# Segment-recurrent attention: Q, K and softmax worked in place, 23 streamed weight pieces, the mask added by a matmul

## The chip, the cores and the metric

The kernel runs on one core of a Trainium2 chip. The metric is device time in microseconds. The kernel before takes 1896.9 us, the median of three runs from 1884.9 to 1905.76. Five engines of the core matter here: TensorE (PE in the profile, its weight loads PEld), VectorE (DVE), ScalarE (ACT), GpSimd (POOL), and SyncE (SP), which only issues transfers. Sixteen DMA engines move the data.

## The reference

Two independent attentions on 2048 rows of 640 columns each, with outputs side by side. Part A is a dilated sliding window: 32 heads of 20, each row attends to 8 rows at distance 2. Part B, which the change concerns, is recurrent over 64 segments of 32 rows:

```python
for s in range(n_seg):                       # 64 segments of 32 rows
    h = concat([mem, x[segment s]])          # 8 memory rows + 32 rows = 40
    q, k, v = h @ Wq, h @ Wk, h @ Wv         # 32 heads of 192
    scores = where(mask, q @ k.T * Dh**-0.5, -1e9)
    o = softmax(scores) @ v
    o = o @ Wo                               # back to 640 columns
    mem = o[:8]; outs.append(o[8:])
```

The mask lets memory rows see all 40 rows, and other rows see rows up to themselves. A segment needs the first 8 output rows of the segment before it, so the 64 segments run one after the other. Wq, Wk, Wv and Wo are 640 x 6144 in bf16, 7.9 MB each, more than the on-chip memory holds together.

## The kernel before, in words

**Stages.** Part A runs first (line 24), with part B's resident weights loading beside it. Then 64 segments of part B. In the end project_late (line 782) makes the outputs for the last 8 rows of each segment, which are computed one segment late.

**Weights.** They are cut into pieces: 5 for each of four head groups of q, k and v (128 x 1536, 384 KB), and 24 for the output (128 x 1280, 320 KB). Most stay in SBUF for the whole of part B. Those named in STREAMED (line 285) do not fit: 8 of k, 10 of v and 6 of o, 24 in all, are read from device memory anew in each segment, through a ring of seven buffers, one transfer a piece, issued by SyncE in the order of use (fetch, line 434). A transfer is issued when the piece seven places ahead in the ring has been used.

**Rows.** In a segment the current 32 rows stand in HX as "main"; "ahead" holds the last 8 rows of four coming segments, which are independent of the recurrence. Each k and v group is projected from "ahead" once in four segments (RENEW, line 288) and q for one group a segment (token ql); such a group gets a second pass of 20 matmuls, and its four sets of 8 late columns are kept in small blocks (Lb) until their segment.

**One segment** runs through four head groups. Order on TensorE, VectorE, ScalarE and SyncE is written out by hand, as a list of tokens (ORDER, line 297); each engine takes its own instructions from the tokens in that order. The tokens, for a group g:

- q.g, k.g, v.g: projections (line 512), 20 matmuls of 384 columns, four side by side in the array, into one of three PSUM "acc" buffers.
- e.: copies acc out of PSUM as bf16 (line 518), on ScalarE (S) or VectorE (V) by EVACUATE, into one of three "sb" buffers.
- T.: VectorE transposes 32 x 32 blocks from sb into the columns 0 to 31 of each head third of QT or KT (line 522), while POOL puts the late columns into 32 to 39 (lines 538, 554). There is one QT and one KT, which all groups use in turn.
- S.g: scores, 16 small matmuls into a bank of PSUM (line 573).
- sb.g: VectorE scales the scores, adds the mask and writes them to an SBUF tile t (line 580). mx.g: maximum. sub.g: subtract it and take exp on ScalarE (lines 591, 592). send.g: sum, reciprocal, and the products that write P (lines 596, 597, 606).
- tp.g: P transposed by two matmuls with the identity (line 613). PT.g: VectorE multiplies it with a 0/1 column pair "own" (line 619).
- ve.g: values out of PSUM to Vst, and of a second pass to LV (lines 562, 564). mix.g: P times values (line 632). ot.g: to OT (line 640), by HEADS.
- out.g.h: the output projection of groups 0 to 2, accumulated in Y (line 660); last: that of group 3 (line 687).
- tx: the next segment's rows into HX. ql, eql, Tql: the q projection of the late rows. part, join, close: the halves of Y added, and the next segment's memory rows written into HX (line 694), with which q.0 of the next segment begins. The output rows leave by POOL's queue (line 697).

A PSUM buffer, QT or KT is written anew when the last reader of its former content is done.

Of the kernel before, what the change touches and what calls it, by code (L numbers as in the profile page):

```python
# [23 lines left out]
def part_a(ctx, tc, A_x, A_wqkv, A_wo, out, ident, emit_loads):  # L24
# [241 lines left out]
    with tc.manual_schedule(engines={mybir.EngineType.PE, mybir.EngineType.DVE, mybir.EngineType.Activation}):  # L266
# [4 lines left out]
        for b in range(-1, n_blk):  # L271
# [13 lines left out]
STREAMED = {"q": ((), (), (), ()), "k": ((0, 2), (2, 3), (1, 4), (0, 4)), "v": ((0, 3), (0, 2), (1, 2, 4), (0, 2, 4)),  # L285
            "o": (8, 13, 16, 18, 22, 23)}
SLOT = 1536
RENEW = {0: ("k0", "v2"), 1: ("k1", "v3"), 2: ("k2", "v0"), 3: ("k3", "v1")}
BLOCKS = 18
FIRST = """  # L290
    q.0 e.q0 T.q0 k.0 e.k0 T.k0 q.1 e.q1 k.1 S.0 sb.0 T.q1 e.k1 mx.0 sub.0 T.k1 send.0 q.2 e.q2 v.0 ve.0
    S.1 sb.1 tp.0 PT.0 T.q2 k.2 e.k2 T.k2 mx.1 sub.1 mix.0 ot.0 v.1 ve.1 send.1 S.2 sb.2 out.0.0 out.0.1
    tp.1 mx.2 sub.2 PT.1 q.3 e.q3 T.q3 k.3 send.2 e.k3 T.k3 mix.1 ot.1 v.2 ve.2 tp.2 PT.2 out.1.0 S.3
    sb.3 mx.3 sub.3 out.1.1 mix.2 ot.2 send.3 v.3 ve.3 out.2.0 tp.3 PT.3 tx out.2.1 part mix.3 ot.3 join
    ql eql last close Tql
# [21 lines left out]
def part_b(ctx, tc, B_x, B_mem0, B_Wq, B_Wk, B_Wv, B_Wo, out, ident, n_seg, pre, nbuf, mid):  # L317
# [26 lines left out]

    copied = {}

    def copy_streamed():

        for m, g in need:
            for u in pieces(m, g):  # L350
                if streamed(u):
                    copied[u] = dpool.tile([128, unit_cols(u)], BF16, name="wcopy_%s%d_%d" % u)[:]
                    nc.sync.dma_start(two_rows(copied[u], u), unit_src(u))
# [4 lines left out]
    for m, g in need:  # L358
        resident += [u for u in pieces(m, g) if not streamed(u)]
    res, wait = {}, set()  # L360

    def place_resident(pool, units):
        for u in units:
            res[u] = pool.tile([128, unit_cols(u)], BF16, name="wres_%s%d_%d" % u)[:]

    def load_resident(units):
        for u in units:
            nc.sync.dma_start(two_rows(res[u], u), unit_src(u))

    n_pre, used = 0, 0  # L370
    while n_pre < len(resident) and used < pre:
        used += 2 * unit_cols(resident[n_pre])
# [49 lines left out]
    qk_sb = pool("b_qk", bufs=3)  # L422
# [11 lines left out]
    def fetch(u):  # L434
        t = wstream.tile([128, SLOT], BF16, tag="ws")
        nc.sync.dma_start(t[:, 0:unit_cols(u)], copied[u])
# [485 lines left out]
```

## Time and profile before

| | |
|---|---|
| median of three runs | 1896.9 us |
| the profiled execution | 1895.51 us |
| its span, first to last instruction | 1893.5 us |
| TensorE busy | 1650.9 us, 87% |
| VectorE busy | 1243.6 us, 66% |
| ScalarE busy | 714.6 us, 38% |
| GpSimd busy | 687.2 us, 36% |
| moved by DMA | 649.28 MB |

Busy is the time in which an engine has an instruction of its own in work. Matmul ends are modelled in the profile, so that TensorE's busy time is somewhat generous. The DMA digits of the page give the mean busy share of the 16 DMA engines in forty equal slices of the span, in tenths, 9 meaning 90% or more. A line of waits names the waiting engine and line, an arrow, what ended the wait, and then the total in us, how often, and the longest. "issue" stands where the profile shows nothing that the engine waited for. A line of operations gives count, busy time, mean time of one in ns, and the engine's idle time just before.

### The profile page before, as it was taken

The page shows a single profiled execution, that of the slowest core. Times are in us where ns is not written, and L with a number is a line of the kernel's source. Part 1 is how long each engine was busy: PE and PEld are TensorE (multiplying, and loading weights), DVE is VectorE, ACT ScalarE, POOL GpSimd, SP SyncE. Part 2 cuts the span into 40 slices and gives each one's busy share as a digit, 9 for nine tenths or more (in the row PEclk, how much of TensorE's full clock was granted, in tenths as well). Part 3 has the DMA queues.
Part 4 walks back from the last instruction along what each step waited for, and adds up shares of the span by engine and source line. Part 5 has one row for each costly group of instructions (what it writes and reads, how often), then busy time and mean ns, then how long its engine had stood idle before and what let it go on. Part 6 is the DMA issues. An engine that isn't in the chain of part 4 may idle for free.

```text
span 1893.5 us, 91779 instructions
## 1 busy us (share of the span) xinstructions
PE 1650.9 (87%) x39286; PEld 1031.8 (54%) x39286; DVE 1243.6 (66%) x3544; ACT 714.6 (38%) x1820; POOL 687.2 (36%) x1864
## 2 busy tenths in 40 slices
PE   8897898888898888888888888888888898888878
PEld 5565555555555555555555555555555555555558
DVE  4786676666666666667667667667666676666630
ACT  4454333334343333333333333343333333333320
POOL 3001344343343434433434334344443344444320
PEclk9999999999999999999999999999999999999999
DMA  9927899999999999999999999999999999999991
GB/s 328 320 72 262 312 379 364 360 358 365 373 366 368 360 369 360 358 361 364 357 364 368 365 340 369 365 360 366 373 371 366 358 382 365 343 365 368 356 370 45
DMA packets 286356, 649.28 MB, mean 343 GB/s; under 512 B 61140, under 2 KB 76946, under 8 KB 285948
## 3 DMA queue, kind: packets, MB, share of 16 engines
q1 hardware_dynamic: 267036, 630.01, 91.8%
q0 software_dynamic: 18400, 13.08, 2.2%
q8 instruction: 308, 5.05, 1.1%
q14 instruction: 100, 0.82, 0.1%
q10 hardware_dynamic: 512, 0.33, 0.1%
HBM read 629.10 MB, written 23.24 MB: 345 GB/s over the span
## 4 chain that ended last, share of the span: by engine, by line
PE 60%; DMA 22%; DVE 8%; issue 5%; ACT 3%; SPq 1%; ACTq 0%; POOL 0%; DVEq 0%
PE acc L512 33%; DMA t<-wcopy_v 13%; PE Y L660 6%; PE px L573 5%; DMA t<-wcopy_k 4%; DMA t<-wcopy_o 4%; PE px L632 3%; PE px L687 3%; PE pq L95 3%; PE px L613 2%; PE px L796 1%; DVE prod L151 1%; ACT part L667 1%; PE po L161 1%; ACT OT L640 1%
## 5 line engine op out<-in xcount | busy, mean ns | idle before, releaser
L512 PEld LDWEIGHTS <-HX 128*32 128x32 bf16 x19380 | 494.1, 97 | 416.7 <-issue 132.0
L512 PE MATMUL acc<-t,HX 128*32 128x384 bf16 x5812 | 434.2, 331 | 51.4 <-DMA t<-wcopy_v 30.5
L518 ACT CAST sb<-acc 128x384 bf16<-128x384 f32 x562 | 256.9, 476 | 429.9 <-PE acc L512 405.1
L512 PE MATMUL acc<-wres_q,HX 128*32 128x384 bf16 x6460 | 331.8, 330 | 58.9 <-DVE HX L694 43.5
L512 PE MATMUL acc<-wres_k,HX 128*32 128x384 bf16 x3876 | 246.0, 329 | 6.3 <-issue 5.9
L554 POOL COPY QT<-Lb 128x96 bf16<-128x96 bf16 x252 | 67.6, 268 | 476.0 <-PE px L573 475.8
L512 PE MATMUL acc<-wres_v,HX 128*32 128x384 bf16 x3232 | 225.6, 328 | 4.7 <-issue 4.6
L660 PE MATMUL Y<-wres_o,OT 128*32 128x320 bf16 x3840 | 212.0, 305 | 6.4 <-issue 6.0
L641 POOL COPY OL<-OT 128x96 bf16<-128x96 bf16 x256 | 157.8, 617 | 149.9 <-ACT OT L640 73.0
L619 DVE TENSOR_TENSOR PT<-px,own 128x320 bf16<-128x320 f32 x256 | 125.1, 489 | 105.6 <-PE px L613 51.9
L640 ACT CAST OT<-px 128x240 bf16<-128x240 f32 x384 | 126.1, 365 | 179.6 <-PE px L632 142.7
L592 ACT ACTIVATE t<-t 128x160 f32<-128x160 f32 x256 | 86.1, 336 | 242.1 <-DVE t L591 240.5
L562 ACT CAST Vst<-acc 128x384 bf16<-128x384 f32 x256 | 123.6, 483 | 142.8 <-PE acc L512 71.6
L642 POOL DMA_DIRECT2D late_o<-OL x256 | 139.4, 544 | 81.5 <-POOL OL L641 74.2
L522 DVE STREAM_TRANSPOSE QT<-sb 128x384 bf16<-128x384 bf16 x256 | 146.6, 573 | 17.0 <-PE px L573 14.6
L573 PE MATMUL px<-KT,QT 64*64 64x40 bf16 (+1 forms) x4096 | 139.2, 189 | 19.7 <-issue 9.8
L580 DVE SCALAR_TENSOR_TENSOR t<-px,mask 128x160 f32<-128x160 f32 x256 | 80.2, 313 | 110.5 <-PE px L573 104.1
L522 DVE STREAM_TRANSPOSE KT<-sb 128x384 bf16<-128x384 bf16 x256 | 143.8, 562 | 12.1 <-ACT sb L518 12.0
L573 PEld LDWEIGHTS <-QT 64*64 64x64 bf16 (+1 forms) x4096 | 109.3, 109 | 74.3 <-issue 42.1
L660 PEld LDWEIGHTS <-OT 128*32 128x32 bf16 x4608 | 114.6, 97 | 57.9 <-issue 15.7
L640 DVE CAST OT<-px 128x240 bf16<-128x240 f32 x128 | 51.8, 405 | 132.3 <-PE px L632 123.8
L697 POOL DMA_DIRECT2D out_dram<-XS x256 | 129.2, 511 | 22.4 <-DVE XS L695 15.6
(97 smaller groups left out, 2231.8 us busy)
## 6 DMA issues: line engine op xcount, KB each, us to landing
t<-wcopy_v SPq DMA_DIRECT2D x640, 384.0 KB, 6.2
t<-wcopy_k SPq DMA_DIRECT2D x512, 384.0 KB, 5.9
t<-wcopy_o SPq DMA_DIRECT2D x396, 320.0 KB, 5.7
wres_q<-in_B_Wq_dram SPq DMA_DIRECT2D x20, 384.0 KB, 7.9
late_o<-OL POOLq DMA_DIRECT2D x256, 24.0 KB, 5.1
wres_q<-late_o SPq DMA_DIRECT2D x16, 384.0 KB, 7.3
wres_o<-in_B_Wo_dram SPq DMA_DIRECT2D x18, 320.0 KB, 7.5
wres_k<-in_B_Wk_dram SPq DMA_DIRECT2D x12, 384.0 KB, 8.0
```

The lines of the kernel that those rows point to most:

```text
L512: nc.tensor.matmul(ps[n][32 * j:32 * j + 32].rearrange("p (f n) -> p f n", n=32), lhsT=X[:, dc, :], rhs=columns(w, m, j), start=(dc == 0), ...
L518: copy(sb[:], p[:])
L522: nc.vector.transpose(dst, sb[:].rearrange("p (f n) -> p f n", n=32))
L562: S_(Vst[:], ps[-1][:])
L573: nc.tensor.matmul(Sps[64 * h:64 * h + 64, a, :], lhsT=QT[k0:k1, L * f:L * f + 64], rhs=KT[k0:k1, f, :], start=(outer == 0 and a == 0), st ...
L592: nc.scalar.activation(t1[:], t1[:], ACTF.Exp)
L619: nc.vector.tensor_tensor(PT[:], pt.rearrange("p l (h n) -> p (l h) n", h=2)[:, :, 0:L].unsqueeze(2) .to_broadcast([128, 4, 2, L]), own[:] ...
L640: copy(OT[:, 6 * r:6 * r + 6].rearrange("p c n -> p (c n)"), ps[r][:, 0:6 * L])
L641: nc.gpsimd.tensor_copy(OL[:, g % 2].rearrange("p n c -> p c n"), OT[:, :, 32:L])
L642: nc.gpsimd.dma_start(late_o[s // 4][:, g, s % 4], OL[:, g % 2].rearrange("p n c -> p (n c)"))
L660: nc.tensor.matmul(Y[t:t + 32].rearrange("p (b c) -> p b c", b=2), lhsT=OT[:, slot(c), 0:32], rhs=wide(w, r, gv), start=(i == 0), stop=(i ...
L697: nc.gpsimd.dma_start(out2[SEG * s:SEG * s + SEG - M, Dm + 160 * j:Dm + 160 * j + 160], Ysb[32 * j + M:32 * j + SEG])
```

## The change

- One piece of the output weights less is streamed: 23 pieces (8 of k, 10 of v, 5 of o), others than before. The memory for the resident one comes from what follows: one sb buffer in place of three, 16 late blocks in place of 18, no tile t.
- Q and K are worked in place: the evacuation writes columns 0 to 31 of QT or KT themselves, and VectorE transposes them there. Only a second pass still goes through sb.
- The softmax is worked in place in the PSUM bank of the scores. The mask is added by one matmul more at the head of each score block: identity times mask, broadcast over four heads. The scale moves into the exp. Token sb is gone.
- PT of groups 0, 1 and 2 is made by two ScalarE activations with a scale column (SPREAD), that of group 3 by VectorE as before. The second pass of the values is copied by VectorE in place of ScalarE.
- part uses QT in place of the tile t. The written order, EVACUATE and HEADS are new. In the order ql now stands between mix.3 and last.
- quarter() and PARTS allow pieces that are streamed in part; PARTS is empty, so that every piece is whole.

```diff
-STREAMED = {"q": ((), (), (), ()), "k": ((0, 2), (2, 3), (1, 4), (0, 4)), "v": ((0, 3), (0, 2), (1, 2, 4), (0, 2, 4)),
-            "o": (8, 13, 16, 18, 22, 23)}
+STREAMED = {"q": ((), (), (), ()), "k": ((0, 4), (1, 4), (0, 1), (0, 3)), "v": ((0, 1), (0, 3, 4), (0, 3, 4), (1, 3)),
+            "o": (8, 12, 17, 18, 22)}
+PARTS = {}
-BLOCKS = 18
+BLOCKS = 16
 ORDER = """
-    q.0 e.q0 T.q0 k.0 e.k0 T.k0 q.1 k.1 S.0 sb.0 e.q1 T.q1 k.2 mx.0 e.k1 q.2 T.k1 S.1 sub.0 e.k2 send.0
-    e.q2 sb.1 T.k2 v.0 q.3 mx.1 tp.0 ve.0 PT.0 e.q3 sub.1 v.1 T.q2 mix.0 ve.1 ot.0 S.2 send.1 k.3 tp.1
-    out.0.0 v.2 T.q3 sb.2 mx.2 sub.2 e.k3 out.0.1 PT.1 send.2 tp.2 T.k3 mix.1 ot.1 PT.2 S.3 ve.2 sb.3
-    v.3 mx.3 mix.2 sub.3 send.3 out.1.0 tx out.1.1 tp.3 ql ve.3 ot.2 out.2.0 PT.3 eql out.2.1 mix.3 part
-    ot.3 last join close Tql
+    q.0 k.0 e.q0 T.q0 k.1 e.k0 q.1 T.k0 S.0 e.q1 mx.0 T.q1 e.k1 v.0 T.k1 q.2 sub.0 ve.0 send.0 S.1 k.2
+    tp.0 e.q2 mx.1 e.k2 sub.1 v.1 T.k2 q.3 PT.0 send.1 mix.0 T.q2 tp.1 ve.1 ot.0 S.2 k.3 out.0.0 PT.1
+    e.q3 e.k3 T.q3 v.2 out.0.1 mx.2 mix.1 sub.2 T.k3 S.3 send.2 ve.2 tp.2 ot.1 mx.3 PT.2 v.3 sub.3
+    out.1.0 mix.2 out.1.1 send.3 tp.3 ot.2 PT.3 out.2.0 ve.3 tx out.2.1 mix.3 part ot.3 ql join last eql
+    close Tql
 """
-EVACUATE = {"k0": "SS", "k1": "SS", "k2": "SS", "k3": "VS", "q0": "SV", "q1": "VS", "q2": "VS", "q3": "VS"}
-HEADS = ("SS", "SS", "VS", "SV")
+EVACUATE = {"k0": "VS", "k1": "SS", "k2": "VS", "k3": "SS", "q0": "VS", "q1": "SV", "q2": "SS", "q3": "VS"}
+HEADS = ("SV", "SS", "SV", "VS")
+SPREAD = "SSSV"
...
-    qk_sb = pool("b_qk", bufs=3)
+    qk_sb = pool("b_qk", bufs=1)
...
-    def turn(dst, sb):
-        nc.vector.transpose(dst, sb[:].rearrange("p (f n) -> p f n", n=32))
+    def turn_in_place(t):
+        nc.vector.transpose(t, t)
...
+    def evacuate(m, ps, copies):
+        sb = to_sb(ps[0], copies[0]) if len(ps) > 1 else None
+        copies[1](columns_of(m, 0, 32), ps[-1][:].rearrange("p (f n) -> p f n", n=32))
+        return sb
...
-            S_(LV[g][:], ps[0][:])
+            V_(LV[g][:], ps[0][:])
...
     def scores(g):
         Sps = bank()[:, 0:4 * L].rearrange("p (a n) -> p a n", n=L)
+        nc.tensor.matmul(Sps[:], lhsT=ident, rhs=mask[:].unsqueeze(1).to_broadcast([128, 4, L]), start=True, stop=False)
...
-                                     start=(outer == 0 and a == 0), stop=(outer == 1 and a == 3),
+                                     start=False, stop=(outer == 1 and a == 3),
...
-    def soft_begin(Sps):
-        t1 = one.tile([128, 4, L], FP32, tag="t1")
-        nc.vector.scalar_tensor_tensor(out=t1[:], in0=Sps, scalar=scale,
-                                       in1=mask[:].unsqueeze(1).to_broadcast([128, 4, L]),
-                                       op0=ALU.mult, op1=ALU.add)
-        return t1
...
-        nc.scalar.activation(t1[:], t1[:], ACTF.Exp)
+        nc.scalar.activation(t1[:], t1[:], ACTF.Exp, scale=scale)
...
+        if SPREAD[g] == "S":
+            for b in range(2):
+                nc.scalar.activation(PT[:, :, b], pt.rearrange("p l (h n) -> p (l h) n", h=2)[:, :, 0:L], ACTF.Copy,
+                                     scale=own[:, b:b + 1])
+            return PT
...
-        part = one.tile([128, 4, L], FP32, tag="t1", name="part")[:].rearrange("p a n -> p (a n)")
+        part = QT[:, 0:320].bitcast(FP32)
```

Line numbers of the kernel after differ: the projections are its line 551, the scores 615, the mask's matmul 609, the transposes 560, the copies into QT and KT 589.

More of the change, by code (lines that the diff above doesn't have):

```diff
@@ L350, in copy_streamed @@
             for u in pieces(m, g):
-                if streamed(u):
+                if u in PARTS:
+                    copied[u] = dpool.tile([128, stream_cols(u)], BF16, name="wcopy_%s%d_%d" % u)[:]
+                    load_quarters(copied[u], u, range(PARTS[u]))
+                elif streamed(u):
                     copied[u] = dpool.tile([128, unit_cols(u)], BF16, name="wcopy_%s%d_%d" % u)[:]
@@ L358, in part_b @@
     for m, g in need:
-        resident += [u for u in pieces(m, g) if not streamed(u)]
+        resident += [u for u in pieces(m, g) if not streamed(u) or u in PARTS]
     res, wait = {}, set()
@@ L512, in project32 @@
                     nc.tensor.matmul(ps[n][32 * j:32 * j + 32].rearrange("p (f n) -> p f n", n=32), lhsT=X[:, dc, :],
[L513 removed]
+                                     rhs=columns(w, (m, g, dc), j), start=(dc == 0), stop=(dc == 4), tile_position=(0, 32 * j))
         return ps
```

134 lines of the change are left out of this document (81 added, 53 removed).

## The prediction

> **What bounds the kernel now.** I read the page from the top, then the windows, then the period of one segment, then who waits for whom. First the page: span, busy line, DMA share in forty slices, and the engines' shares of the chain that ended last.
>
> ```profile
> span 1893.5 us, 91779 instructions
> PE 1650.9 (87%) x39286; PEld 1031.8 (54%) x39286; DVE 1243.6 (66%) x3544; ACT 714.6 (38%) x1820; POOL 687.2 (36%) x1864
> DMA  9927899999999999999999999999999999999991
> PE 60%; DMA 22%; DVE 8%; issue 5%; ACT 3%; SPq 1%; ACTq 0%; POOL 0%; DVEq 0%
> ```
>
> Two resources are nearly full: TensorE by its busy time, the DMA engines in every slice of part B. The windows view for 200 to 1800 us gives both exactly (columns: length; PE, PEld, DVE, ACT, POOL busy; clock; DMA share; GB/s).
>
> ```profile
> 200.00:1800.00 1600.00, 1403.10 (x34826) 856.35 (x34822) 1091.15 (x3333) 614.12 (x1613) 642.58 (x1751) 0.99 1.00 363
> ```
>
> The DMA share is 1.00 at 363 GB/s: the DMA engines never rest. TensorE is busy 87.7%. The clock is not in play (0.99). One instruction comes once in a segment, the add that writes the next segment's memory rows into HX (line 694), and its first and last start give the period:
>
> ```profile
> L694 DVE TENSOR_TENSOR HX<-Vst,KT x63: 199/199/241, 215.8 to 1800.7; 128x40 bf16<-128x40 f32 x63
> ```
>
> (1800.7 - 215.8) / 62 = **25.56 us a segment**. Next SyncE's own waits and TensorE's, both for 300 to 1800 us, that is 1500 / 25.56 = 58.7 segments (total us, times, longest):
>
> ```profile
> SPq L436 <- PE acc L512: 626.0, 720, 3.4
> ```
> ```profile
> PE acc L512 <- DVE HX L694: 40.1, 58, 0.7
> PE px L687 <- ACT OT L640: 39.5, 59, 0.7
> PE acc L512 <- issue: 25.3, 40, 1.3
> PE acc L512 <- DMA t<-wcopy_v: 20.2, 50, 1.0
> PE px L573 <- issue: 9.8, 9, 1.9
> PE acc L512 <- DMA t<-wcopy_k: 8.1, 15, 1.3
> PE px L632 <- issue: 8.0, 11, 1.3
> PE Y L660 <- issue: 7.7, 12, 1.6
> PE acc L512 <- DVE HX L493: 5.2, 20, 0.3
> ```
>
> SyncE waits for a weight buffer to come free, so all seven are nearly always in flight or in use; that and the share of 1.00 say that the streamed weights set the period. But TensorE's waits for weights are only (20.2 + 8.1) / 58.7 = 0.48 us a segment, and its unexplained "issue" stalls (25.3 + 9.8 + 8.0 + 7.7) / 58.7 = 0.87 us. Without both, its path would be 25.56 - 0.48 - 0.87 = **24.2 us**. So TensorE stands 1.4 us behind the DMA bound: whatever lowers the one can be worth no more than that before the other takes over.
>
> **The change part by part, in us a segment.**
>
> *24 pieces become 23.* One piece of the output weights stays in SBUF.
>
> ```profile
> t<-wcopy_o SPq DMA_DIRECT2D x396, 320.0 KB, 5.7
> ```
>
> 327,680 B at 363 GB/s is 0.90 us. The DMA floor becomes 25.56 - 0.90 = **24.66**. Over 62 periods that is -56 us, the most that this part can give.
>
> *TensorE's path.* Durations now: blocks from the chain in order of time (start, us, what), operations from the groups by form for 300 to 1800 us (busy, mean ns).
>
> ```profile
> 1007.17 4.25 PE acc L512 x100
> 1011.42 0.50 PE px L573 x16
> 1003.53 0.84 PE Y L660 x24
> 1017.23 0.45 PE px L632 x16
> ```
> ```profile
> L518 DVE CAST sb<-acc 128x384 bf16<-128x384 f32 x72 | 40.2, 558 | 26.3 <-PE acc L512 26.2
> L522 DVE STREAM_TRANSPOSE QT<-sb 128x384 bf16<-128x384 bf16 x234 | 134.1, 573 | 14.3 <-PE px L573 12.0
> L522 DVE STREAM_TRANSPOSE KT<-sb 128x384 bf16<-128x384 bf16 x233 | 131.0, 562 | 11.1 <-ACT sb L518 11.1
> L587 DVE TENSOR_REDUCE mx<-t 128x4 f32<-128x160 f32 x234 | 69.9, 299 | 4.1
> L591 DVE TENSOR_TENSOR t<-t,mx 128x160 f32<-128x160 f32 x235 | 74.8, 318 | 4.0
> L592 ACT ACTIVATE t<-t 128x160 f32<-128x160 f32 x235 | 79.1, 336 | 222.1 <-DVE t L591 220.6
> L596 DVE TENSOR_REDUCE sm<-t 128x4 f32<-128x160 f32 x235 | 74.8, 318 | 53.3 <-ACT t L592 51.0
> L597 DVE RECIPROCAL sm<-sm 128x4 f32<-128x4 f32 x235 | 41.8, 178 | 8.0
> L606 DVE TENSOR_TENSOR P<-t,sm 128x128 bf16<-128x128 f32 x235 | 68.8, 293 | 8.1
> L606 DVE TENSOR_TENSOR P<-t,sm 128x32 bf16<-128x32 f32 x235 | 44.1, 187 | 0.0
> L580 DVE SCALAR_TENSOR_TENSOR t<-px,mask 128x160 f32<-128x160 f32 x234 | 73.3, 313 | 93.1 <-PE px L573 87.4
> L619 DVE TENSOR_TENSOR PT<-px,own 128x320 bf16<-128x320 f32 x236 | 115.3, 489 | 97.2 <-PE px L613 48.5 <-PE px L632 45.1
> L640 DVE CAST OT<-px 128x240 bf16<-128x240 f32 x118 | 47.7, 405 | 124.0 <-PE px L632 116.0 <-PE Y L660 7.5
> L613 PE MATMUL px<-ident,P 128*128 128x128 bf16 x470 | 69.0, 226 | 2.5 <-DVE P L606 1.3
> L667 ACT COPY part<-Y 64x160 f32<-64x160 f32 x118 | 33.9, 288 | 28.1 <-PE Y L660 27.4
> ```
>
> A projection group of 20 matmuls is 4.25 / 5 = 0.85; one q, k or v group in four has a second pass, so I add 0.21 where k or v stands.
>
> (a) **Mask by matmul: +0.3.** Four more matmuls of 128 weight columns. Nearest is L613: 69.0 / 470 = 0.147 each in a row, 0.226 alone; nothing if it runs inside a wait. Bounds 0 to 0.9. It reads neither QT nor KT, so at S.1 and S.2 it runs inside the waits of (c); I take 0.15 at S.0 and S.3 alone. The step that it replaces (L580, 4 x 0.313) leaves VectorE and the softmax chain.
>
> (b) **ql behind mix.3: -0.67.** The last projection used to wait for OT (39.5 / 58.7 = 0.67). Now the 20 matmuls of ql (0.85) lie between, longer than the wait. The 0.09 of HX L493 goes too, since those rows are turned earlier than ql now comes.
>
> (c) **In-place Q and K: new waits.** Three sb buffers let a group be copied out of PSUM before the scores of the group ahead had run. Now the copy writes QT or KT itself, so copy and transpose both follow the scores. From S.0 to S.1 VectorE does the copy of q1 0.558, mx.0 0.299, the turns of q1 0.573 and k1 0.562, with a hand-over of some 0.04 each (estimated): 2.15, and a fourth of 0.57 for renewed late rows: 2.29. TensorE has v.0 and q.2 beside it: 0.85 + 0.21 + 0.85 = 1.91. **Wait 0.38.** To tp.0: 0.318 + 0.336 + 0.318 + 0.178 + 0.293 + hand-overs, 1.65, against S.1 and k.2, 0.50 + 0.85 + 0.21 = 1.56: 0.1. From tp.0 to S.2: mx, sub, turn of k2, send, turn of q2 with hand-overs 3.05, renewal 0.28, against tp, v.1, q.3, mix.0, tp.1 at 0.29 + 1.06 + 0.85 + 0.45 + 0.29 = 2.94: **0.39.** From S.2 to tp.2: turns of q3 and k3, mx, sub, send, 2.73, hand-overs 0.36, the copy of q3 (0.5) and the rest of PT.1 before it, renewal 0.14, some 4.1, against k.3 1.06, out.0 0.84, v.2 1.06, mix.1 0.45, S.3 with mask 0.65, 4.06: 0.1 with rounding. Before out.2.0 the VectorE half of ot.2 (0.405) stands behind the softmax end that also feeds tp.3; tp.3 covers about half: 0.25. What is queued behind a waiting score block is every later projection, and SyncE's fetches wait for those. Together **+1.2**, with bounds 0 (all of it in time that TensorE lost to weights) and 2.6 (renewals and hand-overs twice as dear).
>
> (d) **PT on ScalarE, three groups of four: 0.** Two activations of 160 elements lie between 2 x 0.288 and 2 x 0.336 by L667 and L592, against 0.489 on VectorE. For groups 0 and 1 the cover is q.3 and k.3 with v.2; ScalarE is busy 38%. For group 2 the exp of group 3 queues behind it; v.3 and out.1.0 cover that, and without cover it is 0.2. [...]
>
> (e) **Scores stay in PSUM for the softmax: 0.** L580 reads PSUM in 313 ns, L591 reads SBUF in 318, same size. Nothing shows a VectorE write to PSUM in the loop. Bounds from the widest gap between comparable rows, 336 - 288 = 48 ns, either way, on 20 steps: -1.0 to +1.0.
>
> (f) The second value tile goes to VectorE, evacuations change sides: VectorE loses L580 (1.25) and three PTs (1.47) and takes back under 1 us, so it stays lighter. POOL fills the same columns; at 36% busy it is hidden by its own waits for the scores. SyncE keeps its order, one issue fewer; the load of XS still stands behind the pieces of v.2. Part A keeps its orders; the head loads one resident piece more and copies one fewer: 0. The last wait of all, HX after the last projection (40.1), stays.
>
> **Sum.** TensorE's path: 24.2 + 0.3 - 0.67 - 0.09 + 1.2 = **24.94**; the DMA floor 24.66. They lie 0.3 apart, too near to hide in each other wholly, and the path leaves out issue stalls of 0.87; I let a fifth of those stay (my choice), 0.17: **25.1**. Against 25.56 that is -0.46 x 62 = -28 us, and 1895.51 (the profiled execution, 2.0 over its span and 1.4 under the median of 1896.9) becomes 1867; against the median **1868**.
>
> **Rivals.**
>
> 1. *The DMA floor is reached* (new waits fall into time that weights cost before): 24.66, -56 us, **1840**. For: SyncE waits for TensorE, so every TensorE wait lets the ring refill. Against: 0.48 us of weight waits cannot hide all of 1.2.
> 2. *The gain is eaten:* the issue stalls (0.87) stay whole on top of the path of 24.94, less what overlaps with the new waits; 25.4 to 25.7, **1885 to 1905**. For: they are as large as the DMA saving. Against: a saturated DMA ring is the only thing that grows beside them.
> 3. *The handover becomes the clock, slower:* scores, copy, turn, scores run serially through VectorE's in-order queue. If (c) comes out at its upper end of 2.6, the period is 25.1 + 1.4 = 26.5 and the time 1895.5 + 0.94 x 62 = **1954**; at 2.1 it is 1923. It decides from (c) = 2.0, where the period passes 25.86. For: VectorE already has 66% and nearly no pause between S.0 and tp.0. Against: three steps out of four there have measured rows.
> 4. *PSUM in place is dear:* +48 ns on 20 steps adds 0.96: 26.06, **1926**. Against: L580 and L591. [...]
>
> That the change does not do what it says (23 pieces without effect) would need a DMA share under 1.00, which the windows exclude.
>
> **How the numbers follow.** Forecast 0.44, rival 1 0.12, rival 2 0.24, rival 3 0.13, rival 4 0.07. A measurement here tells about 1% from no change, so faster means under 1878, slower over 1916. Faster: rival 1 and all but a rim of the forecast, 0.52. Same: rival 2 and that rim, 0.28. Slower: rivals 3 and 4, 0.20. The range goes from the DMA floor, 1840, to 1930, leaving about 2 in 10 out. The forecast's own range is 1852 to 1884.
>
> **What would show it.** DMA share still 0.97 or more with a period near 25.1; the wait of the last projection for OT gone; new TensorE waits before the scores L615 for KT or QT transposes, about 0.4 a segment twice; VectorE's busy share near 60%; in-place subtraction near 318 ns. The prediction is wrong if the new waits of (c) pass 2.0 us a segment together, if the in-place steps take 360 ns or more, or if the issue stalls vanish with the lighter DMA.

## The result, and the profile after

The changed kernel takes 1916.7 us, the median of four runs from 1914.1 to 1925.4; the kernel before took 1901.3 us beside it. The ratio is **1.011**, with a 95% interval from 1.0065 to 1.0155: slower by some 20 us (21 by the ratio, 15 by the two medians), where 28 us faster was forecast. The page of the profiled execution, first its span, busy times, DMA slices and the shares of the chain that ended last:

```profile
span 1912.3 us, 91996 instructions
...
PE 1687.2 (88%) x39542; PEld 1054.1 (55%) x39542; DVE 1148.4 (60%) x3242; ACT 758.6 (40%) x2058; POOL 672.5 (35%) x1864
...
DMA  9927899999999999999999999999999999899991
...
PE 59%; DMA 18%; DVE 8%; POOL 6%; issue 5%; ACT 1%; SPq 1%; ACTq 0%; DVEq 0%; POOLq 0%
```

DMA has gone from 22% of the chain to 18%, and POOL, which had 0%, stands at 6%. The windows view of the stretch that was read before (length; PE, PEld, DVE, ACT, POOL busy; clock; DMA share; GB/s):

```profile
200.00:1800.00 1600.00, 1421.33 (x34684) 868.44 (x34680) 987.34 (x3002) 649.60 (x1824) 622.19 (x1735) 0.99 0.97 346
```

The DMA engines no longer run all the time: 0.97 at 346 GB/s after 1.00 at 363. The period comes from the HX add, now line 731:

```profile
L731 DVE TENSOR_TENSOR HX<-Vst,KT x63: 199/199/307, 218.3 to 1821.3; 128x40 bf16<-128x40 f32 x63
```

(1821.3 - 218.3) / 62 = **25.85 us a segment** after 25.56; 0.29 x 62 = 18 us, the whole loss. TensorE's waits from 300 to 1800 us, 58.0 segments (total us, times, longest):

```profile
PE acc L550 <- DVE HX L731: 40.0, 58, 0.8
PE acc L550 <- issue: 25.8, 36, 2.2
PE acc L550 <- DMA t<-wcopy_v: 21.8, 45, 1.3
PE acc L550 <- DVE sb L556: 16.8, 12, 3.8
PE px L723 <- issue: 13.0, 15, 1.9
PE px L615 <- POOL QT L596: 8.2, 11, 2.2
PE px L615 <- DVE KT L560: 7.0, 15, 0.5
PE Y L697 <- issue: 6.1, 9, 1.0
PE px L672 <- issue: 5.3, 8, 1.2
```

Three things are to be seen. The wait of the last projection for OT (39.5 us before) is gone. The stalls marked issue and the waits for weights are all still there. And there are new waits at the head of a segment: sb (few, but up to 3.8 us), and QT from POOL, up to 2.2 us. With all rows of issue and of weights added up, small ones too, the period divides so (us a segment; "rest", called TensorE's path below, is the period less both: its work and its other waits):

| kernel | period | issue | weights | rest |
|---|---|---|---|---|
| before | 25.56 | 0.89 | 0.54 | 24.13 |
| after | 25.85 | 0.93 | 0.43 | 24.49 |

TensorE's own path grew by 0.36, and the stalls, which the change was forecast to lift nearly wholly, fell by 0.07 of 1.43. The groups by form for the changed steps, 300 to 1800 us (busy, mean ns, idle before):

```profile
L656 ACT ACTIVATE PT<-px,own 128x160 bf16<-128x160 f32 x348 | 119.6, 402 | 3.4 <-PE px L648 2.9 <-ACT OT L680 0.3
...
L626 DVE TENSOR_TENSOR px<-px,mx 128x160 f32<-128x160 f32 x232 | 75.2, 324 | 5.5
L622 DVE TENSOR_REDUCE mx<-px 128x4 f32<-128x160 f32 x232 | 72.1, 311 | 65.1 <-PE px L615 65.1
...
L631 DVE TENSOR_REDUCE sm<-px 128x4 f32<-128x160 f32 x232 | 70.6, 304 | 47.7 <-ACT px L627 47.7
L627 ACT ACTIVATE px<-px 128x160 f32<-128x160 f32 x232 | 68.9, 297 | 130.9 <-DVE px L626 129.5
...
L609 PE MATMUL px<-mask,ident 128*128 128x160 bf16 x231 | 55.7, 241 | 0.8 <-issue 0.8
```

### The profile page after: what moved, and what is told of

Read it like the earlier page. It is cut to its first block, busy times and chain, and to the rows that moved or that the text cites. A ratio compares the mean times of both kernels' runs of the same rounds, so it can differ in the third digit from the quotient of the medians.

```text
span 1912.3 us, 91996 instructions
## 1 busy us (share of the span) xinstructions
PE 1687.2 (88%) x39542; PEld 1054.1 (55%) x39542; DVE 1148.4 (60%) x3242; ACT 758.6 (40%) x2058; POOL 672.5 (35%) x1864
## 3 DMA queue, kind: packets, MB, share of 16 engines
q8 instruction: 310, 5.08, 1.0%
## 4 chain that ended last, share of the span: by engine, by line
PE 59%; DMA 18%; DVE 8%; POOL 6%; issue 5%; ACT 1%; SPq 1%; ACTq 0%; DVEq 0%; POOLq 0%
PE acc L550 30%; DMA t<-wcopy_v 12%; PE Y L697 6%; PE px L615 5%; PE px L672 4%; PE pq L95 3%; POOL out_dram L734 3%; DMA late_o<-OL 3%; DMA t<-wcopy_o 3%; PE px L723 2%; PE px L648 2%; PE px L838 1%; POOL Lb L580 1%; PE px L609 1%; PE po L161 1%
## 5 line engine op out<-in xcount | busy, mean ns | idle before, releaser
L560 DVE STREAM_TRANSPOSE QT<-QT 128x384 bf16<-128x384 bf16 x256 | 146.8, 573 | 133.4 <-ACT QT L589 133.2
L589 ACT CAST KT<-acc 128x384 bf16<-128x384 f32 x256 | 122.8, 480 | 233.8 <-PE px L615 143.1
L550 PE MATMUL acc<-wres_v,HX 128*32 128x384 bf16 x3232 | 206.6, 333 | 3.5 <-issue 2.5
L589 ACT CAST QT<-acc 128x384 bf16<-128x384 f32 x192 | 93.6, 487 | 173.0 <-PE acc L550 154.8
L615 PE MATMUL px<-KT,QT 64*64 64x40 bf16 (+1 forms) x4096 | 139.4, 189 | 25.1 <-POOL QT L596 8.8
L560 DVE STREAM_TRANSPOSE KT<-KT 128x384 bf16<-128x384 bf16 x256 | 142.8, 558 | 22.4 <-ACT KT L589 21.4
L680 ACT CAST OT<-px 128x240 bf16<-128x240 f32 x320 | 109.5, 365 | 102.9 <-PE px L672 101.7
L680 DVE CAST OT<-px 128x240 bf16<-128x240 f32 x192 | 77.6, 404 | 100.9 <-PE Y L697 54.6
L627 ACT ACTIVATE px<-px 128x160 f32<-128x160 f32 x256 | 76.1, 297 | 148.1 <-DVE px L626 146.7
L656 ACT ACTIVATE PT<-px,own 128x160 bf16<-128x160 f32 x384 | 132.0, 402 | 3.4 <-PE px L648 2.9
L672 PE MATMUL px<-PT,Vst 64*128 64x80 bf16 (+1 forms) x2048 | 123.0, 213 | 3.9 <-issue 2.5
```

The lines of the kernel that those rows point to most:

```text
L550: nc.tensor.matmul(ps[n][32 * j:32 * j + 32].rearrange("p (f n) -> p f n", n=32), lhsT=X[:, dc, :], rhs=columns(w, (m, g, dc), j), start=( ...
L560: nc.vector.transpose(t, t)
L589: copies[1](columns_of(m, 0, 32), ps[-1][:].rearrange("p (f n) -> p f n", n=32))
L615: nc.tensor.matmul(Sps[64 * h:64 * h + 64, a, :], lhsT=QT[k0:k1, L * f:L * f + 64], rhs=KT[k0:k1, f, :], start=False, stop=(outer == 1 and ...
L656: nc.scalar.activation(PT[:, :, b], pt.rearrange("p l (h n) -> p (l h) n", h=2)[:, :, 0:L], ACTF.Copy, scale=own[:, b:b + 1])
L672: nc.tensor.matmul(ps[r][lo:hi, 2 * L * k:2 * L * k + 2 * L], lhsT=V[64 * r:64 * r + 64, col:col + hi - lo], rhs=PT[64 * r:64 * r + 64, 2 ...
```

## The experiments

A ratio is to the kernel before on the same chip, with its 95% interval.

**Is the DMA share of 1.00 a floor, and what is a transfer worth?** In two kernels 8 transfers a segment are left out, in a third one; the projections then use another piece's weights in their place.

```diff
 def fetch / get_unit, before_light and after_light (8 pairs), before_23 (one pair)
+ALIAS = {("o", 23, 0): ("o", 21, 0)}
+        u = ALIAS.get(u, u)
```

> The kernel before with eight of its 24 transfers left out in the same way. TensorE's path alone, by the prediction 24.2 or less: 1790 to 1815. If it came near 25.5, TensorE and not the DMA engines would have set the time before.

> The changed kernel with eight of its 23 transfers a segment left out (those pieces are read from another resident piece, so the products are not the reference's; TensorE's work is the same). It shows TensorE's path without the DMA bound: floor 15 x 0.95 = 15 us of transfers. Theory H (waits of the in-place order rule): the period stays at 25.3 or above, time over 1875. Theory D (the path is some 24.5, and the rest comes from transfers that come late because the ring of seven runs full where TensorE waits and empty after): 24.3 to 24.8, 1815 to 1850.

> The kernel before with one of its 24 transfers left out (output piece 23 is read from another resident piece; products not the reference's). The DMA part of the change alone. If the DMA engines set the period of the kernel before, it falls by 0.90 to 24.7: about 1843. If TensorE's path is as near as the prediction had it (24.2), 0.5 to 0.9: 1843 to 1865. Above 1885 the DMA engines were not the bound.

Measured: before_light 1760.8 us, ratio 0.926 [0.920, 0.932]; after_light 1781.8 us, 0.937 [0.931, 0.944]; before_23 1887.1 us, 0.9925 [0.9892, 0.9958]. The HX adds of before_light and of after_light, then TensorE's only waits of the two kinds in the segments of before_light:

```profile
L696 DVE TENSOR_TENSOR HX<-Vst,KT x63: 199/200/239, 210.0 to 1672.9; 128x40 bf16<-128x40 f32 x63
```
```profile
L733 DVE TENSOR_TENSOR HX<-Vst,KT x63: 199/200/276, 210.2 to 1696.6; 128x40 bf16<-128x40 f32 x63
```
```profile
PE px L575 <- issue: 1.7, 1, 1.7
PE px L634 <- issue: 0.9, 2, 0.6
PE acc L514 <- issue: 0.2, 1, 0.2
```

With light transfers the periods are 23.60 and 23.97: the change's own path is **0.37 us longer** than that of before, and both kinds of stall nearly vanish together (0.05 and 0.13 us a segment are left, all issue). Both kernels are faster than was expected of them; the 0.95 us a transfer in the expectation of after_light stands in no run, and by 363 GB/s a piece of 320 KB takes 0.90 and one of 384 KB 1.08, an estimate. Eight transfers are worth 1.96 us a segment, 0.25 each; 1.4 of it are stalls. Of the other 0.6 some 0.16 is the granted clock, 0.994 in place of 0.987 (an estimate from TensorE's 22.4 us of busy time a segment); the remainder is not explained. One transfer is worth 0.0075 of 1901 = 14 us, 0.23 a segment, a quarter of the 0.90 that its bytes took at 363 GB/s. Windows of before_23, 300 to 1700 us:

```profile
300.00:1700.00 1400.00, 1229.39 (x30672) 755.34 (x30671) 961.81 (x2940) 541.35 (x1422) 567.34 (x1540) 0.99 0.99 354
```

The share stays at 0.99 while the rate falls from 363 to 354 GB/s. So the engines moved less and were busy as long: the share counts the time of packets under way, and 0.99 of it was not a limit on bytes here. The kernel before_ql, further down, shows it from the other side: with all 24 transfers it has a period of 25.21 and moves 369 GB/s, at the same share of 1.00. So 25.56 was no floor for 24 transfers, and the 24.66 that was worked out from it was none for 23; a transfer less shortens the period a little at a time.

**What are the issue stalls, and does the ring's depth set them?** The ring of seven buffers was made five in both kernels (two v pieces fewer are streamed, as they fit now), and nine in the changed one (three resident output pieces left out, their neighbours used in their place). S stands in the expectations for the theory that the period is TensorE's own path plus the stalls. Their 1.27 and 1.39 for the issue stalls are not the 0.89 and 0.93 of the table above, and how they were counted isn't on record.

```diff
-nbuf=7,
+nbuf=5,    (before_ring5, after_ring5)      nbuf=9,    (ring9)
```

> The kernel before with five ring buffers in place of seven and, in their memory, two value pieces resident: 22 transfers a segment. Output as the reference's. Theory S with a price of 0.23 a transfer (as one transfer less gave): 25.1, about 1868, if the shallower ring costs nothing. Theory I (TensorE's instruction blocks wait behind the ring's backlog): the issue stalls fall from 1.27 to under 0.9 and weight waits rise by less. If depth matters for the weights, waits for t rise by over 1 us a segment: above 1900.

> The changed kernel with five ring buffers and two value pieces more resident: 21 transfers a segment. Output as the reference's. By the same price 25.4, about 1888, if the shallower ring costs nothing; theory I: issue stalls from 1.39 to under 1.0. If depth matters: above 1916.

> The changed kernel with nine ring buffers in place of seven; the memory comes from three output pieces that are read from a neighbour's place (their products are not the reference's; as many transfers a segment and as many matmuls). Theory D: more depth lets the DMA engines work through TensorE's waits, the period falls by 0.5 us or more: 1885 or less. Theory H: within 8 us of 1916.

Measured: before_ring5 1971.2 us, 1.0386 [1.0351, 1.0421]; after_ring5 1939.6 us, 1.0226 [1.018, 1.0272]; ring9 1912.3 us, 1.0081 [1.0047, 1.0114]. The largest waits for weights of before_ring5, and of ring9 the largest of the issue rows (it has no row for weights):

```profile
PE acc L512 <- DMA t<-wcopy_k: 84.3, 149, 2.4
PE acc L512 <- DMA t<-wcopy_v: 39.3, 57, 1.9
```
```profile
PE acc L552 <- issue: 40.5, 45, 2.3
PE px L725 <- issue: 25.3, 18, 3.0
PE Y L699 <- issue: 13.0, 16, 1.7
```

| kernel | period | issue | weights | rest |
|---|---|---|---|---|
| before, 5 buffers, 22 transfers | 26.68 | 0.04 | 2.29 | 24.35 |
| after, 5 buffers, 21 transfers | 26.10 | 0.10 | 1.72 | 24.28 |
| after, 9 buffers, 23 transfers | 26.16 | 1.63 | 0 | 24.53 |

(The profiled run of ring9 took 1922.7 us, 10 more than its median.) One kind of stall takes the place of the other: in the changed kernel with five, seven and nine buffers the waits for weights are 1.72, 0.43 and 0, the issue stalls 0.10, 0.93 and 1.63. A deeper ring brought no gain, against the 1885 or less that one theory expected, and a shallower one lost time. The trace points to a cause of the issue stalls: instructions arrive by DMA too, on a queue that the page names so (the changed kernel's DMA queues: packets, MB, share):

```profile
q8 instruction: 310, 5.08, 1.0%
```

5.08 MB / 310 are blocks of 16 KB. TensorE starts 260 instructions between two arrivals in the median, weight loads included. All 75 issue stalls of TensorE's matmuls from 300 to 1800 us of the changed kernel end 1.2 to 1.7 us after such a block has arrived (median 1.40); of moments taken evenly, 8% do so, and of TensorE's other waits 10%. In the kernel before it is again 75 of 75, median 1.42. The inference from these times is that TensorE had run out of instructions and waited for their block. That the block stands behind the weights until then is inferred too, from the light kernels and the ring's depth: its own transfer takes 1.0 us with a stall and without one. The issue stalls are 0.05 and 0.13 us a segment with light transfers, 0.89 before and 0.93 after with seven buffers, and 1.63 in ring9.

**The steps one by one.** Five kernels concern single steps of the change, three of them built on the kernel before. The letters in the expectations: S, what shortens TensorE's path shortens the period; B, the DMA engines set the period; M, the mask's matmuls stand whole on the path; P, the waits at the head of a segment rule; H, the in-place order of copy and turn rules.

```diff
 before_ql: ORDER of before, ql and eql moved
-    ... tp.3 ql ve.3 ot.2 out.2.0 PT.3 eql out.2.1 mix.3 part ot.3 last join close Tql
+    ... tp.3 ve.3 ot.2 out.2.0 PT.3 out.2.1 mix.3 part ot.3 ql last join eql close Tql
 before_pad: mask's matmul as mere extra work in scores()
+        nc.tensor.matmul(Sps[:], lhsT=ident, rhs=mask..., start=True, stop=True)
 before_psum: mask by matmul, scores stay in PSUM
+        nc.tensor.matmul(Sps[:], lhsT=ident, rhs=mask..., start=True, stop=False)
-        nc.vector.scalar_tensor_tensor(out=t1[:], in0=Sps, scalar=scale, ...)
-        return t1
+        return Sps
-        nc.scalar.activation(t1[:], t1[:], ACTF.Exp)
+        nc.scalar.activation(t1[:], t1[:], ACTF.Exp, scale=scale)
 nomask: the changed kernel, the mask left out
-        nc.tensor.matmul(Sps[:], lhsT=ident, rhs=mask..., start=True, stop=False)
 mask_tiles: the changed kernel, the mask in two 64x64 tiles
-        nc.tensor.matmul(Sps[:], lhsT=ident, rhs=mask..., start=True, stop=False)
+        for h in range(2):
+            nc.tensor.matmul(Sps[64 * h:64 * h + 64], lhsT=ident[64 * h:64 * h + 64, 64 * h:64 * h + 64],
+                             rhs=mask[64 * h:64 * h + 64]..., start=True, stop=False, tile_position=(64 * h, 64 * h))
```

> The kernel before with one part alone: in the written order ql stands between mix.3 and the last projection. Theory S (the period is TensorE's own path plus some 2 us of stalls for weights and for instruction blocks that come through the same DMA engines; what shortens the path shortens the period): the wait of the last projection for OT (0.67) goes, 1857 to 1870. Theory B (the DMA engines set the period, the path hides under it): within 8 us of the kernel before.

> The kernel before with the mask's matmul put ahead of each score block as mere work: the scores overwrite it, VectorE's mask step stays. TensorE's path grows by the 0.68 us a segment that the matmul took in the changed kernel, nothing else moves. Theory S: up to +42 us, 1925 to 1940. Theory B: under +10 us.

> The kernel before with one part alone: scores stay in PSUM, the mask by a matmul, scale in the exp, no VectorE step with the mask; Q and K, pieces and order as before. Theory M: TensorE's path grows by 0.68 a segment from 24.2 to 24.9, still under the DMA bound of 25.56 but near it: 1900 to 1912. Theory H or P: the part costs nothing there, since sb buffers and turns are as before, and the shorter softmax chain gives a little: 1890 to 1900.

> The changed kernel without the mask's matmul (the mask is left out of the computation; nothing takes its place). Theory M (the mask's four matmuls stand whole on TensorE's path: a score block takes 0.64 us from its start to the next block's in place of 0.47, four times 0.17 = 0.68 a segment): the period falls from 25.85 to some 25.2 and the time by 40 us, to about 1875. Theory P (waits at the head of the segment rule: one sb buffer that comes free only when GpSimd has copied the late rows, behind its stores): the waits take up most of what the matmuls give, under 12 us is gained, above 1903. Theory H (in-place Q and K: copy and turn after the scores): as P, since VectorE's order after the scores is the same.

> The changed kernel with the mask's matmul cut into two of 64 x 64 at the two corners that the scores use. Theory M, if the 0.17 is the change between a whole-array tile and small tiles: about 0.09 a block is left, 4 x 0.08 x 62 = 20 us less, about 1897. If it is the streaming of 160 columns alone (or P or H rule): within 8 us of 1916.

| run | median us | ratio | interval |
|---|---|---|---|
| before_ql | 1882.5 | 0.9929 | 0.9895 to 0.9962 |
| before_pad | 1904.3 | 1.0044 | 1.0003 to 1.0086 |
| before_psum | 1906.3 | 1.0029 | 0.9993 to 1.0065 |
| nomask | 1916.3 | 1.0080 | 1.0049 to 1.0111 |
| mask_tiles | 1923.5 | 1.0105 | 1.0032 to 1.0177 |

Moving ql gives 13.5 us, a third of the 0.67 x 62 = 42 us that the wait for OT had; S expected 27 to 40, B less than 8. The profile of before_ql has no row for that wait. It has a new one for OT further up, in the output projection of group 2, which ql used to cover, 0.27 us a segment; and its window is the one with 369 GB/s:

```profile
PE Y L660 <- DVE OT L640: 16.1, 32, 0.7
```
```profile
300.00:1700.00 1400.00, 1247.27 (x30874) 759.74 (x30877) 968.00 (x2961) 544.16 (x1432) 567.76 (x1549) 0.99 1.00 369
```

The extra matmul costs 0.17 us a block, 0.68 a segment (the median time from a score block's first matmul to what follows goes from 0.47 to 0.64), and as mere work, in before_pad, it costs 0.44%, 8 us of the 42. There the rest of the period is 0.44 us longer than before, 24.57, and the stalls are 0.36 shorter, 1.07: this longer path took most of its 0.44 out of the stalls. Working the softmax in PSUM is not dear; the group of the subtraction in before_psum stands at 322 ns, against 318 from SBUF:

```profile
L588 DVE TENSOR_TENSOR px<-px,mx 128x160 f32<-128x160 f32 x235 | 75.6, 322 | 4.1
```

In the changed kernel the mask's matmul is worth nothing that these intervals separate (1.008 against 1.011). The waits of nomask tell why:

```profile
PE px L614 <- POOL QT L596: 22.4, 30, 3.0
PE acc L550 <- DVE sb L556: 18.0, 12, 3.5
```

The wait for POOL's late columns grew from 8.2 to 22.4 us, that of the scores for KT from 7.0 to 13.2; all waits but those for issue and weights grew by 0.41 us a segment, the stalls by 0.13. TensorE has less to do there, and waits instead: most of the 0.68 comes back at the hand-over. Two 64x64 tiles shorten the block, to 0.54 from 0.64 where no wait falls into it, some 0.4 us a segment, but the time is no better; the rest of the period is 24.25, 0.24 shorter, and the stalls are 1.67, 0.31 longer.

**Do the two gains add, and what takes them away?** before_ql23 has both, ql moved and one transfer left out (piece 21 used for 23), without anything else of the change. before_order is the kernel before with the new written order; after_oldorder is the changed kernel with the old order (ql behind mix.3); after_sel streams the old choice of pieces; after_sb3 has three sb buffers (output piece 10 is left out, 9 used in its place). The letters here: A, the choice of pieces costs; B, the in-place working; C, the order; D, the one sb buffer.

```diff
 before_order / after_oldorder
+ORDER = (that of the other kernel, with sb. tokens where t is used)
 after_sel
-STREAMED = {"k": ((0, 4), (1, 4), (0, 1), (0, 3)), "v": ((0, 1), (0, 3, 4), (0, 3, 4), (1, 3)), "o": (8, 12, 17, 18, 22)}
+STREAMED = {"k": ((0, 2), (2, 3), (1, 4), (0, 4)), "v": ((0, 3), (0, 2), (1, 2, 4), (0, 2, 4)), "o": (8, 13, 16, 18, 22)}
 after_sb3
-    qk_sb = pool("b_qk", bufs=1)
+    qk_sb = pool("b_qk", bufs=3)
```

> The kernel before with ql behind mix.3 and one transfer of output weights left out (piece 21 is used in place of 23): the two gains without in-place working and without the new order. If they add up (0.9929 and 0.9925): 0.985, 0.981 to 0.990. If they are the same gain taken twice (both fill the same stalls): 0.990 to 0.994.

> The kernel before with the written order of the kernel after (with its sb tokens ahead of mx); three sb buffers, tile t, PT on VectorE, 24 pieces, EVACUATE and HEADS as before. Theory C (the order is what costs) expects 1.01 or more. Theories A, B and D expect what the move of ql alone gave, 0.989 to 0.997.

> The kernel after with the written order of the kernel before, without its sb tokens and with ql behind mix.3 as in after. Theory C expects 0.99 or lower, as the in-place working would then cost nothing. Theory B (copies into QT and KT themselves wait for the scores that still read them) expects 1.015 or more: that order has k.2 and q.2 ahead of S.1 and leaves less work behind the waits. A and D expect near 1.011.

> The kernel after with the streamed pieces of the kernel before (8 of k, 10 of v at their old places, o 8, 13, 16, 18 and 22); everything else as after. Theory A (which pieces are streamed, and so when buffers come free, lets the DMA engines idle between 8 and 13 us of a segment): that dip fills, DMA share 0.99 or more, ratio to before 0.995 or lower. The others (B in place, C order, D the one sb buffer) expect no difference from after, 1.007 to 1.015, and a share of 0.97.

> The kernel after with three sb buffers for the second passes in place of one; the memory comes from one resident output piece that is left out (piece 9 is used in place of 10). Theory D (the one sb buffer, freed by GpSimd behind four stores, holds the renewing segments) expects 1.004 or lower, and the periods of segments that renew k0 and k1 within 0.3 us of the others. A, B and C expect no difference from after, 1.007 to 1.015.

| run | median us | ratio | interval |
|---|---|---|---|
| before_ql23 | 1870.3 | 0.9830 | 0.9794 to 0.9865 |
| before_order | 1915.9 | 1.0088 | 1.0053 to 1.0123 |
| after_oldorder | 1925.4 | 1.0132 | 1.0077 to 1.0188 |
| after_sel | 1926.3 | 1.0135 | 1.0082 to 1.0188 |
| after_sb3 | 1910.5 | 1.0039 | 1.0006 to 1.0073 |

The two gains add: 31 us together. So what the change adds beside them costs 1.011 - 0.983 = 2.8%, some **53 us**. The choice of pieces isn't it (after_sel). The new order by itself costs 1.6% (1.0088 against 0.9929 for the same move of ql). The in-place working in the old order costs 3.0% (1.0132 against 0.983), with mask, PT, one sb buffer and the rest of the change; so it brings the whole loss without the new order, and the two costs do not add to the 2.8% of both together. The division of the periods, as above, tells where the loss lies:

| kernel | period | issue | weights | rest |
|---|---|---|---|---|
| before_ql | 25.21 | 0.81 | 0.73 | 23.67 |
| before_ql23 | 25.21 | 1.07 | 0.50 | 23.64 |
| before_order | 26.04 | 0.69 | 1.05 | 24.30 |
| after_oldorder | 25.92 | 0.73 | 0.36 | 24.83 |
| the changed kernel | 25.85 | 0.93 | 0.43 | 24.49 |

Each row is from one profiled run. From before_ql23 to the changed kernel the period grows by 0.64, 40 us: the stalls fall by 0.21, and TensorE's path is 0.85 longer. So the loss lies in the path, not in transfers that come late. Of the 0.85, 0.26 are other waits of over 0.15 us (1.46 after 1.20), and the mask's matmuls take about 0.68 as work. With the old order it is the same, more so. Only in before_order do the waits for weights grow; its profiled run, 1928.8 us, was the slowest of ten, at a granted clock of 0.978. The waits of before_order and its window of 300 to 1700 us:

```profile
PE acc L512 <- DMA t<-wcopy_v: 23.5, 45, 1.9
PE acc L512 <- DMA t<-wcopy_k: 18.3, 32, 1.8
PE acc L512 <- issue: 14.7, 31, 1.0
PE px L573 <- DVE KT L522: 13.9, 25, 0.9
PE Y L660 <- DMA t<-wcopy_o: 10.4, 31, 1.2
```
```profile
300.00:1700.00 1400.00, 1225.72 (x29976) 757.29 (x29978) 949.35 (x2872) 515.87 (x1390) 552.37 (x1512) 0.99 0.99 358
```

Here the weights come late, though no transfer was added. The DMA share by time after the HX add, worked out from the packets (those under way at an edge make it pass 1 a little), is 1.01 to 1.03 in its first 10 us and 0.94 to 0.98 from 10 to 20. In the changed kernel it is 0.92 to 0.93 from 8 to 12 us and 0.87 at 12, where before has 1.00 to 1.01. This fits a chain in which TensorE, held at the head of a segment, frees no weight buffers, SyncE issues nothing and the DMA engines rest. In the changed kernel that has not cost time in waits for weights, though: they are 0.43 us a segment, after 0.54.

The sb buffer is part of it: three in place of one give 0.7%, with intervals that touch (1.0006 to 1.0073 and 1.0065 to 1.0155). The row of sb (16.8 us) is gone, but a part of its time comes back as a wait for POOL (after_sb3), and the segments that renew k0 and k1 still take 26.4 and 26.3 us, the others 25.7 and 24.9, which D did not expect:

```profile
PE px L617 <- POOL QT L598: 9.7, 12, 2.2
...
PE px L617 <- POOL KT L577: 7.7, 6, 3.1
```

**Is it GpSimd's queue at the head of the segment?** There the four stores of the output rows (0.51 us each) stand ahead of the late copies. act_store issues them on ScalarE; after_store issues them on GpSimd behind send.0 of the next segment.

```diff
 act_store, in close()
-            nc.gpsimd.dma_start(out2[...], Ysb[...])
+            nc.scalar.dma_start(out2[...], Ysb[...])
 after_store: the same four stores, called from step "send" of group 0, and POOL in the written order
+                if g == 0:
+                    store_rows()
```

> The changed kernel with the four output stores of a segment issued by ScalarE in place of GpSimd. Theory P: GpSimd is 2 us earlier at the head of a segment (4 x 0.51), the wait of k.1 behind the copy into sb in every fourth segment (1.2 us) goes, S.0 comes earlier, 0.3 to 0.5 a segment: 1880 to 1895. Theory M and theory H: within 6 us of the changed kernel's 1916.

> The kernel after with the four stores of a segment's output rows issued on GpSimd behind send.0 of the next segment, in place of ahead of the late copies; GpSimd's order is written out too. If the head of the segment (late copies of q0 and k0 and the release of the sb buffer behind four stores of 0.51 us) is what lets the DMA engines idle, TensorE's waits at 3 to 5 us of a segment (0.64 us) vanish, the DMA share rises from 0.97 to 0.99 and the ratio falls from 1.011 to 1.000 or lower. If these waits only take the place of others, the ratio stays within 0.4% of 1.011.

Measured: act_store 1924.1 us, 1.0124 [1.0072, 1.0176]; after_store 1963.0 us, **1.0337** [1.0274, 1.04]. In act_store ScalarE itself is held by the four issues (0.38 us each in the median, 1.6 at most; its copies into QT have a row of 71.1 us in 18 waits for "DMA out_dram<-XS"), and TensorE waits for its copies of q instead, so it doesn't decide:

```profile
PE acc L550 <- ACT QT L589: 26.0, 32, 2.4
```

after_store does what was expected at the head of the segment: TensorE's waits for sb and for POOL there fall from 0.43 us a segment to 0.03. But it is far slower. TensorE's waits for weights in it, and SyncE's two largest:

```profile
PE acc L550 <- DMA t<-wcopy_v: 61.3, 94, 3.2
...
PE Y L697 <- DMA t<-wcopy_o: 17.7, 25, 2.2
```
```profile
SPq L474 <- PE acc L550: 557.6, 618, 3.3
SPq L523 <- DMA out_dram<-XS: 167.3, 94, 6.0
```

L523 is the load of the next rows into XS. It stands in SyncE's queue among the weights, and now waits for the stores out of XS: 167.3 us in 56.5 segments, 3.0 us each, in which no weight is fetched (DMA share 0.63 to 0.68 from 14 to 16 us). So the waits at the head can be taken away, but this run does not tell what that alone is worth; a second XS buffer, which would let the load go ahead of the stores, wasn't tried.

**A version that beats both kernels** is before_ql, the kernel before with ql behind mix.3 and nothing else: 1882.5 us, 0.9929 [0.9895, 0.9962].

## Why the prediction was wrong, point by point

- **The step that failed: "the path leaves out issue stalls of 0.87; I let a fifth of those stay"**, and before it "Without both, its path would be 24.2". The sum took 1.35 us of stalls off the period and put 0.17 back. They stayed: 1.36 after, 1.43 before. The path itself came out *shorter* than forecast: 24.49 against 24.94, or 0.36 longer than before where 0.74 was added up. 24.49 + 1.36 = 25.85 is the measured period. The stalls were not a sum that lies beside the path: where it got shorter, by 0.46 in before_ql and 0.24 in mask_tiles, they grew by 0.11 and 0.31; in before_pad, with a path longer by 0.44, they shrank by 0.36. before_order goes the other way: there both grew, by 0.17 and 0.31.
- **Under it lies the reading of the DMA share.** "The DMA engines never rest" was true of the row and was no floor. before_23 gives 0.23 us a segment for the piece, not 0.90, and eight pieces give 0.25 each; before_ql moves 24 pieces in 25.21. The change thus had 14 us from this part, not up to 56. The prediction took a share of 1.00 as proof that a piece less must have its full effect; it is none.
- (a) The mask's matmul takes 0.68 a segment, not 0.3, inside the bounds of 0 to 0.9. As work alone it costs 8 us; taken out of the changed kernel, it gives nothing that the intervals separate.
- (b) The move of ql removed the wait for OT as said. Alone it gave 13.5 us, not 0.76 x 62 = 47: the new wait for OT before out.2 (0.27 a segment, in before_ql) and 0.11 more of stalls took back half of the 0.76, and the profiled run of before_ql is 9 us faster than its median.
- (c) The waits for in-place QT and KT: rows of sb, QT and KT, (16.8 + 8.2 + 7.0 + 4.6 + 3.5) / 58 = 0.69, against 1.2, and at another place than forecast. S.1 has its 0.5 only in segments that renew k1. The largest are at the head of a segment: the one sb buffer holds TensorE in those that renew k0 (16.8), and POOL's late copies into QT in eleven of the others (8.2). I had written that POOL is "hidden by its own waits for the scores", and left the one sb buffer unpriced. Its hand-overs of some 0.04 were an estimate with no row beside it; in the trace of the kernel before the pause is 0.034 from one VectorE step of the softmax to the next, 0.052 from a projection to its copy and 0.094 from the subtraction to the exp (medians).
- (d) PT on ScalarE takes 402 ns for each half, above the bounds of 288 to 336. The two rows of the bounds, L667 and L592, have no column of scalars as own is, and how much of the difference that column makes was not shown. TensorE's waits have no row for PT.
- (e) In PSUM against SBUF: subtraction 324 against 318 ns, maximum 311 against 299, sum 304 against 318, exp 297 against 336. Right, and rival 4 falls. The three rows of VectorE lie between 12 ns more and 14 less in PSUM, that of ScalarE 39 less.
- Rivals: the DMA floor (1840) is refuted by before_23 and before_ql. The handover as a clock decided from (c) = 2.0 and was not reached. Nearest is the second, "the issue stalls stay whole": it had the stalls right, but with 25.4 to 25.7 it counted on overlap that did not come, so its time of 1885 to 1905 lies below the measured 1916.7.
- Of the signs named: OT's wait gone, VectorE at 60%, the subtraction near 318, the share at 0.97 all came; the period of 25.1 did not, and the new waits of the scores for KT and QT transposes were 0.18 a segment in all, not 0.4 twice. The share at 0.97 was named as a sign of success, and was one of idle DMA engines. None of the three signs of being wrong came: they watched (c), the in-place steps and vanishing stalls, and none of them the stalls that stay.

**What stays open.** The profiles put the 53 us between before_ql23 and the changed kernel in TensorE's path, but they are not divided among the steps. By after_sb3, 0.7% (13 us) hangs on the one sb buffer. The mask's matmuls are 0.68 us of work a segment, yet nomask gives back 0.3% by its ratio, which the intervals do not separate from nothing. What in-place Q and K, PT on ScalarE, the sides of the copies and the 16 late blocks cost, each by itself, was not run. Why the new order alone costs 1.6% on the kernel before stays open too. That held TensorE, freed buffers and idle DMA engines belong together is read from their times within the segment; the run that should have shown it by itself, after_store, ran into SyncE's queue.

## What to carry to other kernels

A DMA share of 1.00 was no proof here that bytes are the limit (0.99 at 354 GB/s in before_23, 1.00 at 369 in before_ql): leave one transfer out and measure what it is worth before a change is built on it. Where, as here, the DMA share is 1.00 and TensorE is busy 88% of the time, count the stalls that are already there as staying: a shorter path gave a third or less of what it saved (before_ql 13.5 us of 42, mask_tiles nothing), and a longer one cost a fifth of what it added (before_pad 8 us of 42). Before a transfer is moved, look who waits for its buffer: in after_store the load of XS waited 3.0 us a segment, and no weight behind it in SyncE's order was fetched in that time.

## What the runs showed of the hardware

- TensorE's stalls without a visible cause end 1.4 us (median) after a block of 16 KB has arrived on the instruction queue, 75 of 75 in each of the two kernels. They are 0.05 us a segment with 16 weight transfers (before_light), 0.9 with 24 and 23 in seven buffers (before and after), 1.6 with nine buffers (ring9).
- The kernel before with a ring of five buffers (before_ring5) has 0.04 us a segment of these stalls and 2.29 of waits for weights, where seven buffers have 0.89 and 0.54; although two transfers fewer are needed, it is slower by 3.9%.
- The DMA share stood at 0.99 to 1.00 at rates from 354 GB/s (before_23) to 369 (before_ql).
- A matmul over the whole array ahead of sixteen small tiles costs 0.17 us in place (a score block takes 0.64 us after, 0.47 before); cut into two 64x64 tiles it costs 0.07 (0.54 in mask_tiles), though each of the two takes 250 ns by the groups, against 241 for the one.
